# A planner's figures for a transfer through DRAM: later landings and twice the bytes

## The chip, the cores and the metric

The kernel runs on one core of one Trainium2 chip. The metric is the device time of one execution in microseconds (us), lower being better.

## The reference

Gated linear attention feeds a two-layer feed-forward network (FFN). With batch 4, 8 heads, 768 steps and head size 48:

```
for t in range(S):
    state = alpha[:, :, t, :, None] * state + k[:, :, t] (outer) v[:, :, t]
    y[:, :, t] = q[:, :, t] . state
x = y as 3072 tokens x 384
h = x @ w_in                      # 384 x 2048
out = gelu(h) @ w_out             # 2048 x 384
```

## The kernel before

**The attention** is cut into 24 units, numbered n = 2g + u: twelve groups g of 256 steps of one batch, and in each two halves u of four heads. For a unit VectorE (DVE) runs scans over alpha (`pp`, `rp`, lines L315 and L328), multiplies queries and keys by them (`qd` L321, `kd` L334), and TensorE (PE) then makes scores (L355), the part inside a chunk (L445), the new states from keys and values (L464) and the part that comes from older states (L514). ScalarE (ACT) copies the finished `y` out of PSUM (`yc`, L594), so that the bank can be written again.

**The keys have to be turned** for L464. In units 0 to 5 TensorE does it. In units 6 to 23 (`n >= FLIPPED`) DVE transposes 32x32 blocks into `fl` (`flipped`, L371), one DMA writes `fl` to DRAM (`fd`, `flip_out`, L378), four DMAs of 64 KB read it back in another order (`kx`, `flip_back`, L384), and ACT copies `kx` into the tile `kn` that TensorE reads (`flip_over`, L392). `fl` and `kx` have one buffer, `kn` two, `fd` two.

**The FFN** works in float32 with split operands: each weight and each activation is a high and a low part, and three products are summed. Groups 0 to 3 are narrow blocks (256 tokens, first product L622, second L714), the others four wide blocks of 512 tokens (L639, L657). Between the two products ACT does the GELU twice (`ghi` L691, and in place, L695), and DVE takes the difference (`glo` L704).

**The order is made by a planner** that runs when the kernel is built. Every step is an `Op` with an engine, a cost, a list of steps that it depends on and a rank. The planner goes through a time of its own: on each engine it places the step of lowest rank whose inputs are ready; when TensorE has no attention step that is ready, it takes an FFN step. The steps are then issued in the planned order on PE, DVE, ACT and the queue of SyncE (SP). On the chip each engine keeps that order and waits for its semaphores, so the planner's figures set the order and nothing else. For a step that issues transfers, the planner takes one shared bus and a landing time:

```
bus[0] = max(bus[0], o.start) + o.kb / RATE
o.end = (max(o.end, bus[0]) if o.kb else o.end) + o.lands
```

`RATE` is 360 (KB per us of its own count), `WAIT` is 0.2 us between engines, and `o.end` in the second line begins as start plus cost (0.35 for `move`, 1.4 for `moves`). A load of a unit counts 786 KB, or 1179 with the values.

For n from 7 to 12 TensorE's order is the trio outer of n - 2 (L514), inside of n - 1 (L445 and L464), scores of n (L355), issued together; its first step is held back until `kn` of n - 1 is planned as ready, and until keys and queries of n are. Later units keep that hold, with the scores second.

Of the kernel before, what the change touches and what calls it, by code (L numbers as in the profile page):

```python
# [47 lines left out]
def gla_then_gelu_ffn(ctx: ExitStack, tc: tile.TileContext, q, k, v, alpha, qg, kg, ag, vg, w_in, w_out, out):  # L48
# [119 lines left out]
    for half in range(2):  # L168
        r = slice(half * CS, (half + 1) * CS)
# [171 lines left out]
    def scores(g, u):  # L341
        d = cur[g, u]
        n = NU * g + u
        d["s"] = s_of(n)
        if n >= SPLIT:
            d["s"] = [
                ps_h().tile([P, BANK], F32, tag="hp", name=f"sh_{n}"),
                ps_w().tile([P, BANK], F32, tag="sw", name=f"sw_{n}"),
            ]
        for j in range(NCH):  # L350
            for i in range(2):
                t, o = slice(j * CS, (j + 1) * CS), slice(i * CS, (i + 1) * CS)
                for h in range(2):
                    r = slice(h * DP, h * DP + D)
                    nc.tensor.matmul(  # L355
                        d["s"][h][o, t], lhsT=d["kt"][r, (2 * j + i) * CS : (2 * j + i + 1) * CS], rhs=d["qt"][r, i, t], start=True, stop=True
                    )

    def turned(g, u):
        d = cur[g, u]  # L360
        for j in range(NCH):
            e = (2 + j % 2) * C
            nc.tensor.transpose(
                out=d["s"][j // 2][:, e : e + C], in_=d["kt"][:, 2 * j * CS : 2 * (j + 1) * CS], identity=ident
            )

    def flipped(g, u):

        d = cur[g, u]
        d["fl"] = work.tile([P, 4, NCH, QUAD], F32, tag="fl", bufs=1, name=f"fl_{g}_{u}")  # L370
        nc.vector.transpose(  # L371
            out=d["fl"], in_=d["kt"].rearrange("p (j i a t) -> p (i a) j t", j=NCH, i=2, a=2)
        )

    def flip_out(g, u):
        d = cur[g, u]
        d["fd"] = bounce.tile([P, 4, NCH * QUAD], F32, tag="fd", name=f"fd_{g}_{u}")
        nc.sync.dma_start(d["fd"], d["fl"].rearrange("p q j d -> p q (j d)"))  # L378

    def flip_back(g, u):  # L380
        d = cur[g, u]
        d["kx"] = work.tile([P, 4, NCH * QUAD], F32, tag="kx", bufs=1, name=f"kx_{g}_{u}")
        for dst in range(4):
            nc.sync.dma_start(  # L384
                d["kx"][dst * QUAD : (dst + 1) * QUAD],
                d["fd"].rearrange("(s t) q e -> q t s e", t=QUAD)[dst],
            )

    def flip_over(g, u):
        d = cur[g, u]  # L390
        d["kn"] = work.tile([P, 2, NCH, 2, QUAD], F32, tag="kn", bufs=2, name=f"kn_{g}_{u}")
        nc.scalar.copy(  # L392
            d["kn"].rearrange("p h j b d -> p h b j d"),
            d["kx"].rearrange("p (h b) (j d) -> p h b j d", h=2, d=QUAD),
        )
# [476 lines left out]
    def op(*args, **kw):  # L872
        ops.append(Op(*args, **kw))
        return ops[-1]
# [4 lines left out]
    def plan_unit(n):  # L879
        g, u = divmod(n, NU)  # L880
        d = unit[n] = {}
        p, pp_ = unit.get(n - 1, {}), unit.get(n - 2, {})
        r = unit_rank[n]
# [24 lines left out]
        of_y = [yp.get("out", yp.get(x)) for x in ("xh", "xl")]  # L908
        if n >= FLIPPED:
            flip = op("DVE", "flip", lambda: flipped(g, u), [d["keys"], p.get("away")], rank=r)  # L910
            d["away"] = op("SP", "move", lambda: flip_out(g, u), [flip], rank=r - 50, lands=2.2, kb=262)
            back = op("SP", "moves", lambda: flip_back(g, u), [d["away"], p["kn"]], rank=r - 50, lands=2.2, kb=262)
            d["kn"] = op("ACT", "over", lambda: flip_over(g, u), [back, pp_["inside"]], rank=-0.5)
            d["scores"] = op("PE", "scores1", lambda: scores(g, u), [d["keys"], d["q"], sp.get("mask"), sp.get("kn") if n < FLIPPED + NU else None, *shared], rank=r)
        else:
            d["scores"] = op("PE", "scores", lambda: (scores(g, u), turned(g, u)), [d["keys"], d["q"], sp.get("mask"), sp.get("kn"), *shared], rank=r)
# [110 lines left out]
    for n in range(n_units):  # L1027
        plan_unit(n)
# [350 lines left out]
```

## Time and profile before

| | us |
|---|---|
| median of 3 runs | 499.61 (498.85 to 500.62) |
| the profiled execution, its own time | 501.89 |
| its span, first to last instruction | 500.3 |

The profiled execution is one of its own: its time lies 1.59 us above its span, and 2.28 us above the median of the three. Its mean granted TensorE clock is 0.994 of full speed. PE was busy for 483.0 us of the span. The page's busy time of PE is modelled from pipelined matmuls, so idle stretches of PE are read as lost time and busy stretches not as peak.

### The profile page before, as it was taken

Reading aid. Unit: us, or ns where it says so; the run is one execution under the profiler, and the core shown is the slowest. Engines: PE = TensorE matmul, PEld = TensorE weight load, DVE = VectorE, ACT = ScalarE, POOL = GpSimd, SP = SyncE. Lnnn points to the kernel's source line nnn. Section 1 sums busy time; section 2 is a strip of 40 time slices with the busy share of each in tenths; the row PEclk is TensorE's granted clock in tenths of the full one; section 3 lists DMA queues with packets and bytes.
Section 4 is the critical chain, followed back from the end, with each engine's and each line's share of the span. In section 5 each row is a group of like instructions: output and inputs, shape, how many; then the busy total and the mean of one; then the engine's idle time right before and its main releaser. Section 6 shows DMA issues by size and latency. Waiting matters only on the chain.

```text
span 500.3 us, 12076 instructions
## 1 busy us (share of the span) xinstructions
PE 483.0 (97%) x5144; PEld 411.6 (82%) x5144; DVE 261.1 (52%) x503; ACT 201.4 (40%) x399; POOL 7.4 (1%) x21
## 2 busy tenths in 40 slices
PE   7899999998988999999999999999999999999994
PEld 5788998998988998988888777888777888888883
DVE  7998999897877897311111988211532121221212
ACT  5788676434354445231313444222432232332321
POOL 2000000000000000000000000000000000000000
PEclk9999999998999999999999999999999999999998
DMA  8996653755655466100000545000210000100001
GB/s 304 393 346 206 234 190 118 222 180 150 181 171 187 132 195 188 58 33 0 1 0 1 184 157 168 17 0 2 90 41 9 0 1 0 64 1 0 1 0 70
DMA packets 33806, 53.76 MB, mean 107 GB/s; under 512 B 4272, under 2 KB 15344, under 8 KB 33744
## 3 DMA queue, kind: packets, MB, share of 16 engines
q1 hardware_dynamic: 32096, 47.86, 29.3%
q0 software_dynamic: 880, 3.93, 2.0%
q10 hardware_dynamic: 768, 1.11, 0.7%
q8 instruction: 42, 0.69, 0.6%
q14 instruction: 20, 0.16, 0.1%
HBM read 41.29 MB, written 9.44 MB: 101 GB/s over the span
## 4 chain that ended last, share of the span: by engine, by line
PE 72%; DMA 11%; DVE 6%; ACT 5%; SPq 2%; issue 2%; ACTq 0%; DVEq 0%
PE hw L639 27%; PE accw L657 27%; PE acc L714 6%; PE hp L622 5%; DMA st<-in_moe_w_out_dram 2%; DMA kd<-in_kg_dram 2%; DMA x<-z 2%; DMA kx<-fd 2%; PE sbank L514 1%; PE sbank L445 1%; DMA vn<-in_vg_dram 1%; DVE rp L328 1%; SPq L209 1%; ACT ghi L691 1%; PE differ L295 1%
## 5 line engine op out<-in xcount | busy, mean ns | idle before, releaser
L704 DVE TENSOR_TENSOR glo<-hw,ghi 128x512 fp32r<-128x512 f32 x64 | 44.1, 690 | 185.9 <-ACT hw L695 185.9
L639 PE MATMUL hw<-x,wih 128*128 128x512 f32 x384 | 120.9, 395 | 0.0
L691 ACT ACTIVATE ghi<-hw 128x512 fp32r<-128x512 f32 x64 | 38.3, 598 | 171.9 <-PE hw L639 171.9
L639 PEld LDWEIGHTS hw<-x,wih 128*128 128x128 f32 x384 | 71.8, 188 | 17.0
L657 PE MATMUL accw<-ghi,woh 128*128 128x512 f32 x192 | 76.2, 397 | 0.0
L639 PE MATMUL hw<-x,wil 128*128 128x512 f32 x192 | 75.8, 395 | 0.0
L657 PE MATMUL accw<-ghi,wol 128*128 128x512 f32 x192 | 75.2, 392 | 0.0
L622 PE MATMUL hp<-x,wih 128*128 128x256 f32 x384 | 69.7, 282 | 0.0
L622 PEld LDWEIGHTS hp<-x,wih 128*128 128x128 f32 x384 | 59.9, 188 | 0.5 <-issue 0.2
L657 PE MATMUL accw<-glo,woh 128*128 128x512 f32 x192 | 56.2, 394 | 0.0
L622 PE MATMUL hp<-x,wil 128*128 128x256 f32 x192 | 53.6, 280 | 0.0
L714 PE MATMUL acc<-woh,ghi 128*128 128x384 f32 x128 | 45.2, 353 | 0.8 <-ACT ghi L691 0.8
L714 PE MATMUL acc<-wol,ghi 128*128 128x384 f32 x128 | 43.6, 341 | 0.0
L639 PEld LDWEIGHTS hw<-x,wil 128*128 128x128 f32 x192 | 36.0, 187 | 8.9
L657 PEld LDWEIGHTS accw<-ghi,woh 128*128 128x128 f32 x192 | 36.0, 188 | 8.5
L657 PEld LDWEIGHTS accw<-ghi,wol 128*128 128x128 f32 x192 | 36.1, 188 | 7.8
L657 PEld LDWEIGHTS accw<-glo,woh 128*128 128x128 f32 x192 | 35.7, 188 | 7.8
L695 ACT ACTIVATE hw<-hw 128x512 f32<-128x512 f32 x64 | 37.9, 593 | 0.0
L622 PEld LDWEIGHTS hp<-x,wil 128*128 128x128 f32 x192 | 36.2, 188 | 0.0
L328 DVE TENSOR_TENSOR_SCAN rp<-ad,rp,bottom 128x255 f32<-128x255 f32 x48 | 33.9, 738 | 0.8
L315 DVE TENSOR_TENSOR_SCAN pp<-ad,bottom 128x256 f32<-128x256 f32 x48 | 30.8, 667 | 3.8 <-DMA ad<-in_ag_dram 3.8
L704 DVE TENSOR_TENSOR glo<-hp,ghi 128x512 fp32r<-128x512 f32 x30 | 20.6, 687 | 20.8 <-ACT hp L695 20.5
(137 smaller groups left out, 575.3 us busy)
## 6 DMA issues: line engine op xcount, KB each, us to landing
st<-in_moe_w_in_dram SPq DMA_DIRECT2D x8, 768.0 KB, 6.1
st<-in_moe_w_out_dram SPq DMA_DIRECT2D x8, 768.0 KB, 7.7
qd<-in_qg_dram SPq DMA_DIRECT2D x23, 256.0 KB, 4.1
ad<-in_ag_dram SPq DMA_DIRECT2D x23, 256.0 KB, 3.8
kd<-in_kg_dram SPq DMA_DIRECT2D x23, 256.0 KB, 4.8
vn<-in_vg_dram SPq DMA_DIRECT2D x12, 416.0 KB, 6.5
fd<-fl SPq DMA_DIRECT2D x18, 256.0 KB, 2.7
kx<-fd SPq DMA_DIRECT2D x72, 64.0 KB, 3.9
```

Of the source, the lines that this page charges most:

```text
L209: eng.dma_start(data[g % NB][name][:, p].rearrange("p a t -> p (a t)"), src[n])
L295: nc.tensor.matmul(d["to"][i], lhsT=ident, rhs=w[:, i], start=True, stop=False)
L315: nc.vector.tensor_tensor_scan(pp[:, i], at[:, i], bottom, MID, ALU.mult, ALU.max)
L328: nc.vector.tensor_tensor_scan(rp[:, i, G - 2 :: -1], at[:, i, G - 1 : 0 : -1], bottom[:, 1:], rp[:, i, G - 1 :], ALU.mult, ALU.max)
L445: nc.tensor.matmul(ybank[o, i, j * CS : (j + 1) * CS], lhsT=vn[r, j, e : e + rows], rhs=d["ss"][r, h, j, :], start=(j == 0 and i not in sp ...
L622: nc.tensor.matmul(hp[:, j, :], lhsT=a[:, j, i * P : (i + 1) * P], rhs=x[:, i, :], start=(start and m == 0), stop=(stop and (j, i, n) in t ...
L639: nc.tensor.matmul(h, lhsT=a[:, j, i * P : (i + 1) * P], rhs=x[:, i, part], start=(i == 0 and n == 0), stop=(i == NK - 1 and n == 2),)
L657: nc.tensor.matmul(acc[i], lhsT=w[:, j, e], rhs=a, start=(f == 0 and k == 0 and w is wo_hi[f2]), stop=(f == NF - 1 and k == 1),)
L691: nc.scalar.activation(ghi, hp, AF.Gelu)
L695: nc.scalar.activation(hp, hp, AF.Gelu)
L704: nc.vector.tensor_tensor(out=glo, in0=hp, in1=ghi.bitcast(F32), op=ALU.subtract)
L714: nc.tensor.matmul(acc[t], lhsT=a[:, j, t * C : (t + 1) * C], rhs=w[:, j, :], start=(first and j == 0 and k == 0 and w is wo_hi[f]), stop= ...
```

## The change

It changes three numbers that the planner is told. No instruction is added, removed or resized. The write to DRAM (`move`) is told to land 2.6 instead of 2.2 after its end on the bus, the four reads (`moves`) 4.5 instead of 2.2, and the reads count 524 instead of 262 KB on the bus.

```
         if n >= FLIPPED:
             flip = op("DVE", "flip", lambda: flipped(g, u), [d["keys"], p.get("away")], rank=r)
-            d["away"] = op("SP", "move", lambda: flip_out(g, u), [flip], rank=r - 50, lands=2.2, kb=262)
-            back = op("SP", "moves", lambda: flip_back(g, u), [d["away"], p["kn"]], rank=r - 50, lands=2.2, kb=262)
+            d["away"] = op("SP", "move", lambda: flip_out(g, u), [flip], rank=r - 50, lands=2.6, kb=262)
+            back = op("SP", "moves", lambda: flip_back(g, u), [d["away"], p["kn"]], rank=r - 50, lands=4.5, kb=524)
             d["kn"] = op("ACT", "over", lambda: flip_over(g, u), [back, pp_["inside"]], rank=-0.5)
             d["scores"] = op("PE", "scores1", lambda: scores(g, u), [d["keys"], d["q"], sp.get("mask"), sp.get("kn") if n < FLIPPED + NU else None, *shared], rank=r)
```

## Rows read from the trace of the kernel before

**Rows 1.** Page, busy time of an engine, its share of the span, instructions.
```profile
PE 483.0 (97%) x5144; PEld 411.6 (82%) x5144; DVE 261.1 (52%) x503; ACT 201.4 (40%) x399; POOL 7.4 (1%) x21
```

**Rows 2.** Busy time by stretch: start:end, length, engines, PE clock, DMA share, GB/s.
```profile
78.00:211.50 133.50, 128.39 (x2189) 122.37 (x2190) 105.98 (x223) 57.66 (x129) 2.33 (x3) 0.99 0.53 163
211.50:493.50 282.00, 281.96 (x1891) 226.46 (x1889) 85.92 (x162) 85.59 (x165) 2.38 (x4) 1.00 0.11 34
```

**Rows 3.** Page, the chain that ended last, share of the span by engine.
```profile
PE 72%; DMA 11%; DVE 6%; ACT 5%; SPq 2%; issue 2%; ACTq 0%; DVEq 0%
```

**Rows 4.** Waits, 78 to 211 us: waiter and releaser, total us, times, longest.
```profile
ACT kn L392 <- DMA kx<-fd: 30.1, 11, 4.0
...
PE ybank L355 <- ACT yc L594: 1.8, 2, 1.0
...
PE sbank L445 <- ACT yc L594: 1.6, 2, 1.4
...
PE sbank L464 <- ACT kn L392: 1.0, 2, 0.5
...
PE sw L355 <- ACT yc L594: 0.8, 1, 0.8
```

**Rows 5.** The same waits, 211.5 to 493.5 us: ACT's copies of turned keys.
```profile
ACT kn L392 <- DMA kx<-fd: 14.4, 4, 5.2
```

**Rows 6.** Instructions of PE in order of time around unit 9's `kn`.
```profile
115.67 0.65 PE L445 MATMUL sbank<-ss,vn 64*64 64x64 f32 x32
116.84 0.68 PE L464 MATMUL sbank<-vn,kn 64*64 64x48 f32 x32 [0.52 <-ACT kn L392]
118.51 1.13 PE L355 MATMUL ybank<-qd,kd 48*64 48x64 f32 x32 [0.99 <-ACT yc L594]
```

**Rows 7.** Instructions of ACT in the same stretch.
```profile
112.97 0.59 ACT L695 ACTIVATE hp<-hp 128x512 f32<-128x512 f32 x1
116.17 0.62 ACT L392 COPY kn<-kx 128x512 f32<-128x512 f32 x1 [2.61 <-DMA kx<-fd]
116.69 0.72 ACT L217 ACTIVATE junk<-ad,hi_b 128x512 uint8<-128x512 f32 x1
117.32 0.19 ACT L217 ACTIVATION_READ_ACCUMULATOR junk<-ad,hi_b 128x1 f32 x1
117.41 0.57 ACT L691 ACTIVATE ghi<-hp 128x512 fp32r<-128x512 f32 x1
117.89 0.57 ACT L594 COPY yc<-ybank 128x512 f32<-128x512 f32 x1
```

**Rows 8.** Busy time by stretch after these two stalls (columns as in group 2).
```profile
117.00:119.00 2.00, 1.01 (x51) 0.88 (x50) 1.15 (x6) 2.00 (x7) 0.00 (x0) 0.89 0.64 215
119.00:121.00 2.00, 2.00 (x28) 1.88 (x23) 1.98 (x4) 1.07 (x4) 0.00 (x0) 0.50 0.74 237
121.00:123.00 2.00, 2.00 (x11) 2.00 (x11) 0.33 (x2) 0.41 (x2) 0.00 (x0) 0.75 0.58 170
```

**Rows 9.** Issues of SP's queue in order of time, unit 9.
```profile
106.77 0.34 SPq L378 DMA_DIRECT2D fd<-fl  x1
107.15 0.43 SPq L209 DMA_DIRECT2D ad<-in_ag_dram  x1
...
108.61 0.43 SPq L211 DMA_DIRECT2D vn<-in_vg_dram  x1
109.14 2.43 SPq L384 DMA_DIRECT2D kx<-fd  x4
```

**Rows 10.** DMA issues: tiles, queue, count, KB each, median us to landing.
```profile
fd<-fl SPq DMA_DIRECT2D x18, 256.0 KB, 2.7
kx<-fd SPq DMA_DIRECT2D x72, 64.0 KB, 3.9
```

**Rows 11.** The same for the tile `kx` alone, its extremes.
```profile
DMA to landing us min/median/max: 1.8/3.9/7.3
```

**Rows 12.** Instructions of ACT around unit 13's `kn`.
```profile
156.74 0.62 ACT L392 COPY kn<-kx 128x512 f32<-128x512 f32 x1 [2.75 <-DMA kx<-fd]
157.26 0.72 ACT L217 ACTIVATE junk<-ad,hi_b 128x512 uint8<-128x512 f32 x1
...
158.98 0.58 ACT L594 COPY yc<-sbank 128x512 f32<-128x512 f32 x1
```

**Rows 13.** Chain that ended last, one FFN step: start, length, what.
```profile
123.03 2.12 PE hp L622 x18
```

## The prediction

> **What bounds the kernel now.** I read the page's busy times first: PE is busy 97% of the span [rows 1], and the chain that ended last is PE for 72% [rows 3]. A change that adds no PE work can then only move what PE stands idle, so the next view is the table by stretch. From 211.5 to 493.5 us PE is busy 281.96 of 282.00 us: nothing is to be won there. From 78 to 211.5 us it is busy 128.39 of 133.50 [rows 2], which leaves 5.1 us of idle time. Most of the turned units are made here, eleven of the fifteen waits of ACT for them among them [rows 4, 5]. The waits of this stretch name the owners of that idle time: 1.0 us in two waits of PE for ACT's `kn` copies, and 1.8, 1.6 and 0.8 us for ACT's `yc` copies [rows 4]. They sum to 5.2, which is all of it. ACT in turn stood 30.1 us waiting for the `kx` transfers, in eleven waits [rows 4], and 14.4 us more in the later stretch [rows 5], where PE lost nothing. So the wait on ACT has no price of its own. It costs only where something that PE needs soon is queued behind it.
>
> Unit 9 shows both ways of paying. PE had issued the first half of inside (L445) and then stood 0.52 us for `kn`, and after that 0.99 us for `yc` before the scores [rows 6]. On ACT the copy of `kn` began at 116.17 after 2.61 us of idling for `kx`; a range check, a GELU and only then `yc` followed, at 117.89 [rows 7]. Had `kx` come 2.6 us earlier, or had the planner put check and GELU in front of `kn`, `yc` would have been done when PE asked. After the two stalls the granted clock fell to 0.89, 0.50 and 0.75 in three stretches of 2 us [rows 8], that is, to its lower level, 1.2 of 2.4 GHz, for part of them. The loss is (0.11 + 0.50 + 0.25) x 2 = 1.7 us. Unit 13 shows the second way alone: `kn` at 156.74 after 2.75 us of idling, a check, and `yc` at 158.98 [rows 12]; this is the longest wait of L445, 1.4 us [rows 4].
>
> **The change part by part.** No instruction is added or removed, so all of it is order. By the two lines that the planner uses, a write issued at 0 landed at 262/360 + 2.2 = 2.93 before, the reads ended max(1.4, 0.73) + 2.2 = 3.6 later, and with the 0.2 between engines the copy `kn` could be placed 6.73 us after the write's issue. Now it is 0.73 + 2.6 = 3.33, then 1.46 + 4.5 = 5.96, so 9.49: the copy moves back by 2.76 us of the planner's time. Where a load with values (1179 KB, 3.28 us of bus) is issued between write and reads, as in unit 9 [rows 9], the bus term decides in place of the 1.4: before 0.73 + 3.28 + 0.73 + 2.2 = 6.94, now 0.73 + 3.28 + 1.46 + 4.5 = 9.97, a shift of 3.03. On the chip unit 9 took 116.17 - 106.77 = 9.40 us from the issue of the write to the copy [rows 7, 9]. The new figure fits this unit to within 0.6, the old one was 2.5 short, and that is about the 2.61 us that ACT idled [rows 7].
>
> What moves with it. (a) On ACT the copy stands later, so GELUs, checks and `yc` copies that are now queued behind it go in front. (b) On PE the trio is held back until `kn` is planned as ready, and PE takes FFN steps meanwhile. One narrow first product is 2.12 us [rows 13], so a hold of 2.8 is one or two such steps. This is work that PE has to do anyway. If no FFN step were left, the hold would cost its full 2.8 us per unit. Against that speaks that PE goes on with narrow blocks (L622) all through this stretch and then with wide ones for 282 us without a gap [rows 2]; there is stock. (c) The planned landing also delays the loads of a later unit, since they wait for the trio that reads their buffers; they are issued one or two FFN steps later. These loads are outside PE's 5.1 us now, and DVE, which needs them, is busy 105.98 of 133.50 us [rows 2], so it has some 27 us to give. If that slack is used up, PE waits for keys instead; that is the rival on the other side below. (d) The extra 262 KB are 0.73 us of planned bus for the transfers that come after; this only repeats (c) in small.
>
> The sum, for the stretch from 78 to 211.5 us:
> - The two waits for `kn`, 1.0 us [rows 4]: they go, because the copy is planned where it really lands. -1.0.
> - The waits for `yc` behind such copies: 0.99 [rows 6], 0.8 (the only wait of `sw`), and the two of L445, 1.6 [rows 4], together 3.4. The second wait of `ybank` L355, 1.8 - 0.99 = 0.8, stands at the start of the stretch ahead of the first `kn`, so the change does not touch it; it also shows that `yc` can be late without `kx`. Bounds: all 3.4 go, or none. I take two thirds, because unit 9's and unit 13's `yc` have check and GELU behind `kn` that can go ahead [rows 7, 12]. -2.3.
> - The clock: 1.7 us [rows 8] if the pair of stalls of unit 9 goes. The profiled execution is 2.28 us above the median of the runs, so the median may hold this only in part. I take half, with bounds 0 and 1.7. -0.9.
> - New stalls. No row shows them. The lower bound is nothing, as in the long later stretch [rows 2], and the upper is the cost of one such pair with its clock, 0.52 + 0.99 + 1.7 = 3.2 [rows 6, 8]. A new order of some hundred steps does not come out without any; I take two of the size of unit 9's first, +1.0.
>
> That makes -3.2 us: 499.61 - 3.2 = 496.4 for the median. Against the profiled execution's own time the clock counts in full, 501.89 - 4.0 = 497.9, with a span near 496.3.
>
> The Trainium skill, "DMA: Bandwidth & Descriptors", section "Anatomy of one DMA", would speak against the change: it gives a transfer a fixed 2.0 us plus its bytes at 436 GB/s (its fit is for another issuing path). By that an estimate for a read of 64 KB is 2.15 us and for the write of 256 KB 2.6 us, so 2.2 would have been right for the reads and 4.5 a needless hold, and the sum would be 0. Here the write's median of 2.7 agrees [rows 10]; the reads' median of 3.9 does not, and only their minimum of 1.8 comes near it, with 7.3 at the other end [rows 11].
>
> **The rivals.**
> - *Paid back, or too late for nothing (no change).* The wait on ACT falls, but PE's idle time only changes its place, as in the later stretch, where 14.4 us on ACT cost PE nothing [rows 5]. For it: only 5.2 of 30.1 us on ACT reach PE [rows 4], and reads that land in 1.8 us [rows 11] make a hold planned for 4.5 empty. Against: the two waits for `kn` are direct. In this case the copy still runs before PE asks, a few stalls of 0.5 to 1 us replace others, and the time is 499.6 give or take 1.2.
> - *The held trio makes keys late (slower).* A trio held back by 2.8 us frees its buffers as much later, the next unit's load goes out as much later, and the scans of DVE start late; then PE stands at the scores (L355) for `kd`. Its price is that of unit 9, stall and clock, 3.2 us each time [rows 6, 8]. If the old stalls go as well (-4.4 and up to -1.7), it takes two such places to come out even and three for +3.5; if the old `yc` stalls stay, one or two are enough, for 501.5 to 503. Against it: DVE's 27 us of slack [rows 2].
> - *Everything goes (much faster).* All of 1.0 + 3.4 + 1.7 = 6.1 us, with no new stall: 493.5.
>
> **How the numbers follow.** Less than 0.3%, 1.5 us, can't be told from no change here: faster is below 498.1 and slower above 501.1. The forecast, 494.5 to 498.1, gets 0.45; everything gone, 0.13; no change, 0.25; keys late, 0.17. So faster is 0.58, same 0.25, slower 0.17. The likeliest time is 496.4. The range begins with the case in which everything goes, 493.5, and ends inside the slower case, at 501.6; some 0.08 is left out below and 0.11 above.
>
> **What would show it.** Right: ACT's idle time for `kx` from 78 to 211 falls from 30.1 to less than 15 us; PE's waits for `kn` are gone and those for `yc` are below 2 us; PE's idle time in the stretch is 2 to 3 us, and the clock is 1.00 from 115 to 125. More FFN steps stand between two trios in units 8 to 12. Wrong: PE waits at L355 for `kd`, or the clock falls in another place (keys late); the idle total stays near 5 us under other names (paid back); or PE shows idle time before an FFN step, which would mean that the stock ran out.

## The result, and the profile after

| | before | after |
|---|---|---|
| median, us | 499.23 (497.68 to 500.62, 4 runs) | 493.60 (493.41 to 493.84, 4 runs) |
| ratio of the times | | 0.9888, 95% interval 0.9858 to 0.9919 |
| span of the profiled execution | 500.3 | 492.1 |

The change made the kernel 1.1% faster, 5.6 us between the medians. The runs of the changed kernel lie within 0.4 us, those of before over 2.9 us.

The page of the changed kernel, busy time by engine:

```profile
PE 480.8 (98%) x5144; PEld 410.2 (83%) x5144; DVE 262.5 (53%) x503; ACT 202.1 (41%) x399; POOL 7.4 (2%) x21
```

Its busy time by stretch (columns as in group 2 of the rows above):

```profile
0.00:78.00 78.00, 73.59 (x1099) 63.84 (x1099) 69.41 (x122) 59.44 (x109) 2.68 (x14) 1.00 0.77 276
78.00:211.50 133.50, 133.50 (x2194) 126.82 (x2195) 108.11 (x224) 58.91 (x131) 3.06 (x4) 1.00 0.53 166
211.50:485.30 273.80, 273.72 (x1854) 219.57 (x1852) 84.31 (x158) 83.79 (x161) 1.66 (x3) 1.00 0.11 34
```

and, as it was not shown above, the first stretch of the kernel before:

```profile
0.00:78.00 78.00, 72.67 (x1066) 62.82 (x1066) 68.51 (x120) 58.13 (x106) 2.67 (x14) 1.00 0.77 276
```

In the stretch from 78 to 211.5 us PE no longer stands idle at all: 133.50 of 133.50, where it was 128.39 [rows 2]. Of the 8.2 us between the two spans, 5.1 are this: 4.4 in waits behind copies of `kn` [rows 4], 0.4 in the wait at the head of the stretch and 0.3 in a wait of an FFN step for `glo`. The clock's 1.7 us [rows 8] are gone as well, and 5.33 - 4.41 = 0.9 us of idle time fell away before 78 us. That makes 7.7. PE's busy time fell by 483.0 - 480.8 = 2.2 us, 0.5 more than the clock's part; no view shows why. The 0.9 us before 78 are no gain of the change: nearly all of that stretch lies ahead of the first turned unit, and in the experiments below the same idle time is anything from 4.0 to 6.0 us.

The waits of the changed kernel, 78 to 211.5 us, hold one row of those of [rows 4]:

```profile
ACT kn L392 <- DMA kx<-fd: 8.2, 4, 3.0
```

ACT idles 8.2 us for the reads instead of 30.1, in four waits instead of eleven, and the four kinds of PE's waits for `kn` and `yc` are gone. Unit 9 again, PE and then ACT in order of time:

```profile
119.29 0.34 PE L714 MATMUL acc<-woh,ghi 128*128 128x384 f32 x1
119.47 0.34 PE L714 MATMUL acc<-wol,ghi 128*128 128x384 f32 x1
119.74 0.67 PE L514 MATMUL ybank<-qd,state 48*48 48x64 f32 x32
120.22 0.65 PE L445 MATMUL sbank<-ss,vn 64*64 64x64 f32 x32
120.69 0.63 PE L464 MATMUL sbank<-vn,kn 64*64 64x48 f32 x32
121.16 0.69 PE L355 MATMUL ybank<-qd,kd 48*64 48x64 f32 x32
```

```profile
116.31 0.60 ACT L691 ACTIVATE ghi<-hp 128x512 fp32r<-128x512 f32 x1 [5.54 <-PE hp L622]
116.80 0.59 ACT L695 ACTIVATE hp<-hp 128x512 f32<-128x512 f32 x1
117.32 0.60 ACT L392 COPY kn<-kx 128x512 f32<-128x512 f32 x1
...
120.53 0.59 ACT L594 COPY yc<-ybank 128x512 f32<-128x512 f32 x1 [0.91 <-PE ybank L514]
```

The trio now stands behind more FFN work (between it and the trio before it 36 products of L622 and 32 of L714, where it was 36 and 12) and runs without a gap. The copy of `kn` begins 3.4 us before PE asks for it (117.32 to 120.69) and is done in 0.6; before, PE stood waiting for it [rows 6]. On ACT a pair of GELUs went ahead of the copy, and `yc` waits for PE's outer step instead of PE waiting for `yc`. The clock through this place is whole, where it was 0.89, 0.50 and 0.75 [rows 8]:

```profile
117.00:119.00 2.00, 2.00 (x17) 2.00 (x17) 1.65 (x3) 1.50 (x4) 0.00 (x0) 1.00 0.65 252
119.00:121.00 2.00, 2.00 (x93) 1.75 (x94) 0.86 (x2) 1.09 (x4) 0.00 (x0) 1.00 0.27 76
121.00:123.00 2.00, 2.00 (x63) 1.93 (x56) 1.50 (x5) 0.83 (x3) 0.00 (x0) 1.00 0.24 64
```

### The profile page after: what moved, and what is told of

The parts are those of the page before. It is cut to its first block, busy times and chain, and to the rows that moved or that the text cites. A ratio compares the mean times of both kernels' runs of the same rounds, so it can differ in the third digit from the quotient of the medians.

```text
span 492.1 us, 12092 instructions
## 1 busy us (share of the span) xinstructions
PE 480.8 (98%) x5144; PEld 410.2 (83%) x5144; DVE 262.5 (53%) x503; ACT 202.1 (41%) x399; POOL 7.4 (2%) x21
## 4 chain that ended last, share of the span: by engine, by line
PE 88%; DVE 5%; DMA 3%; ACT 2%; issue 1%; POOL 1%; ACTq 0%; SPq 0%; POOLq 0%
PE hw L639 27%; PE accw L657 27%; PE acc L714 11%; PE hp L622 10%; DMA st<-in_moe_w_out_dram 2%; PE sbank L445 2%; PE sbank L514 2%; PE sbank L464 1%; PE differ L295 1%; PE sh L355 1%; DVE rp L328 1%; PE ybank L514 1%; DVE st L273 1%; DVE pp L315 1%; PE ybank L355 0%
## 5 line engine op out<-in xcount | busy, mean ns | idle before, releaser
L622 PE MATMUL hp<-x,wih 128*128 128x256 f32 x384 | 69.5, 281 | 0.0
L622 PEld LDWEIGHTS hp<-x,wih 128*128 128x128 f32 x384 | 59.8, 188 | 0.4 <-issue 0.2
L622 PE MATMUL hp<-x,wil 128*128 128x256 f32 x192 | 53.6, 280 | 0.0
L714 PE MATMUL acc<-woh,ghi 128*128 128x384 f32 x128 | 44.1, 345 | 0.8 <-ACT ghi L691 0.8
L714 PE MATMUL acc<-wol,ghi 128*128 128x384 f32 x128 | 43.1, 336 | 0.0
L622 PEld LDWEIGHTS hp<-x,wil 128*128 128x128 f32 x192 | 36.2, 188 | 0.0
L691 ACT ACTIVATE ghi<-hp 128x512 fp32r<-128x512 f32 x32 | 19.1, 596 | 41.4 <-PE hp L622 41.4
```

What stands on the lines that cost most here:

```text
L622: nc.tensor.matmul(hp[:, j, :], lhsT=a[:, j, i * P : (i + 1) * P], rhs=x[:, i, :], start=(start and m == 0), stop=(stop and (j, i, n) in t ...
L691: nc.scalar.activation(ghi, hp, AF.Gelu)
L714: nc.tensor.matmul(acc[t], lhsT=a[:, j, t * C : (t + 1) * C], rhs=w[:, j, :], start=(first and j == 0 and k == 0 and w is wo_hi[f]), stop= ...
```

## The experiments

Two questions were open. Is the late copy of `kn` really what PE paid for, and which half of the new order pays, ACT's or PE's? And is it the size of the shift that counts, or would any new order have gained? "PE idle" below is the length of the stretch from 78 to 211.5 us less PE's busy time in it, "ACT for kx" the wait of ACT's copy in the same stretch, both from one profiled execution; the median and its ratio to the kernel before come from several runs. Where the profiled execution is far from the median (the table at the end has both), its idle time is not that of the median.

**The wait taken away, all orders kept.** The copy of `kn` reads `fl`, a tile that is already in SBUF. The waits of this and the following kernels are shown for the stretch from 78 to 211.5 us, as waiter and releaser, total us, times, longest.

```
-            d["kx"].rearrange("p (h b) (j d) -> p h b j d", h=2, d=QUAD),
+            d["fl"].rearrange("p (h b) j d -> p h b j d", h=2),
```

> The kernel before, in which ACT's copy into kn reads fl instead of kx (the turned keys are then in the wrong places; all transfers still run). The order on PE, DVE and SP is that of the kernel before, so only ACT's wait for the reads is taken away. Theory (the copy waits for transfers that land later than planned, and PE pays for what stands behind it): PE's idle time from 78 to 211 us falls from 5.2 to under 1.5 us, the clock stays at 1.00, and the time is 493.5 to 496. Rival (the gain is luck of a new order, the waits for kx are harmless): PE's waits for yc stay, 498.5 to 500.

Measured: 495.15 us, ratio 0.9903 (0.9870 to 0.9935). PE idle 133.50 - 132.88 = 0.6 us. PE's waits in the stretch:

```profile
PE ybank L355 <- ACT yc L594: 0.3, 1, 0.3
...
PE acc L714 <- DVE glo L704: 0.3, 1, 0.3
```

The order on PE and DVE is that of the kernel before, to the instruction, and nearly the whole gain is there. So its stalls came from the copy's wait for the reads, also those that the trace puts down to `yc`, which does not read `kx`.

**The two halves of the new order, each alone.** Each of the two kernels moves the copies in its plan after it is made, and the order on PE, DVE and SP stays. The fence shows the lines of both kernels together (the comments are not in them): the first kernel, on the plan of before, has the third line and not the fourth; the second, on the plan of the change, has the fourth and not the third. The first never puts a copy behind the step that reads it, so it moves the copies of units 9 and 11 by 2.0 us only.

```
+    for n in range(FLIPPED, n_units):
+        o, first = unit[n]["kn"], unit[n]["inside"]
+        o.start = min(o.start + 2.8, first.start - 0.01)      # plan of before
+        o.start = max(o.start - 2.8, first.start - 1000)      # plan of the change
     plan.sort(key=lambda o: (o.start, o.n))
```

> The plan of the kernel before, with ACT's copies into kn put 2.8 us later in ACT's order alone (never behind inside); PE, DVE and SP keep the order of the kernel before. Theory: PE's two waits for kn stay or grow (1.0 to 2 us), those for yc fall from 3.4 to about 1.5 us, as GELU and check are now ahead of the copy; 496.5 to 498.5. Rival (PE's held trio does all of it): nothing gained, 499 to 501, with PE waiting longer for kn.

Measured: 497.00 us, ratio 0.9934 (0.9910 to 0.9959). PE idle 2.0 us. ACT for kx, and what is left of PE's waits for it:

```profile
ACT kn L392 <- DMA kx<-fd: 2.0, 1, 2.0
...
PE sbank L464 <- ACT kn L392: 1.3, 1, 1.3
...
PE ybank L464 <- ACT kn L392: 0.2, 1, 0.2
```

> The plan of the changed kernel, with ACT's copies into kn put 2.8 us earlier in ACT's order alone; PE, DVE and SP keep the order of the changed kernel. Theory: ACT idles for kx more than 20 us again between 78 and 211 us, PE has no wait for kn, since its trio is held back, and waits for yc of 0.5 to 1.5 us in sum; 494 to 496. Rival (ACT's order does all of it): PE's waits for yc are back at 3 us, 496.5 to 498.5.

Measured: 494.31 us, ratio 0.9898 (0.9845 to 0.9950). PE idle 0.2 us, and

```profile
ACT kn L392 <- DMA kx<-fd: 18.1, 8, 5.4
...
PE acc L714 <- DVE glo L704: 0.2, 1, 0.2
```

ACT's order alone takes away all waits for `yc`, as (a) said, and more of them than expected; but with PE's order of before the copy is now late for PE, with one wait of 1.3 us. PE's held trio alone (with the new order on DVE and SP) takes away both kinds, though ACT idles 18.1 us for `kx`. The two halves don't add up (0.66% and 1.02%, together 1.1%): either takes away most of the stalls, and the held trio leaves less, 0.2 us of idle time against 2.0.

**The three numbers one by one.** In `move` and `moves`: reads 4.5 alone; bytes 524 alone; write 2.6 alone.

> Only the 4.5 for the reads; the write lands at 2.2 and the reads count 262 KB, as before. By the planner's lines the copy moves back 2.3 us of the 2.76. Theory: nearly all of the gain, 493.5 to 495.5. Rival (a chance order): anywhere between 494 and 501, with PE's idle time at other places.

Measured: 495.36 us, ratio 0.9911 (0.9883 to 0.9939); PE idle 0.3, ACT for kx 10.5. As the theory said. (PE idle here is a wait of an FFN step for `glo`.)

> Only the 524 KB for the reads; both landings stay at 2.2. By the planner's lines the copy moves back 0.06 us where no load stands between write and reads (the bus takes 1.46 and the issues 1.4) and 0.73 where one does. Theory: the copies stay far ahead of the transfers, ACT still idles over 20 us for kx between 78 and 211 us, and PE keeps stalls behind them: 497 to 500. Rival (any new order gains, the order of before is an unlucky one): 494 to 496 with ACT's waits unchanged.

Measured: 494.82 us, ratio 0.9895 (0.9860 to 0.9929); PE idle 0.35 us, and

```profile
ACT kn L392 <- DMA kx<-fd: 12.7, 9, 2.8
...
PE ybank L355 <- ACT yc L594: 0.5, 2, 0.3
```

A miss: the bytes alone bring all that can be told from the change itself. Either any new order would do, or a shift of less than 1 us is already enough.

> Only the 2.6 for the write. The copy moves back 0.4 us. Theory: as for the bytes alone, 497.5 to 500, with ACT's waits for kx over 20 us and stalls of PE of 3 us or more between 78 and 211 us. Rival (unlucky order of before): 494 to 496.

Measured: 498.62 us, ratio 0.9982 (0.9954 to 1.0010), no difference that these runs can tell. PE idle 2.0 us, nearly all of it in waits for `yc` (one of 1.0 in unit 9's trio and one of 0.8 in unit 11's), and ACT for kx 27.1. This is hardly a new order, though: the plan puts the copies of units 6 to 11 where they were, because in those units other steps and transfers decide and not the write's landing, and the trace has the order of before on PE, ACT and DVE up to 143 us. Its two waits are there in the kernel before too, of the same length; the two waits for `kn` in front of them (0.5 us each before) are missing in this execution. So the run does not decide between any new order and a short shift.

**The size of the shift, smaller and in the other direction, and a control.** The reads' landing alone at 1.5, 2.6 and 3.0 instead of 2.2; then, with the figures for the keys as before, `lo=1.0` instead of `lo=0.89` in the table of costs.

> Only the reads' landing, at 1.5 instead of 2.2: the copies move 0.7 us the other way. Theory (the margin between copy and trio sets the stalls): PE stalls for kn and yc grow over the 5.2 us of the kernel before, ACT idles over 30 us for kx between 78 and 211 us, 499.5 to 502.5. Rival (any new order gains): 494 to 497.

Measured: 502.53 us (498.66 to 503.98), ratio 1.0046 (1.0011 to 1.0080): half a per cent slower. The profiled execution took 500.30, 2.2 below the median, with PE idle 3.5 us in the stretch and 1.4 us behind it (a wait of a wide block's second product for a GELU, at 290 us), so the stalls of 5.2 or more were not seen. What the other executions lost shows in part in the granted clock: its mean over the span is 0.994 or less in five of the seven, and 0.988 or 0.989 in three, where the profiled one has 0.998. ACT for kx rose as expected:

```profile
ACT kn L392 <- DMA kx<-fd: 37.4, 13, 6.7
...
PE ybank L355 <- ACT yc L594: 1.7, 3, 1.0
...
PE sw L355 <- ACT yc L594: 1.5, 1, 1.5
...
PE sbank L464 <- ACT kn L392: 0.6, 2, 0.3
```

> Only the reads' landing, at 2.6 instead of 2.2, a shift of the copies of 0.4 us. Theory: part of the gain, PE's stalls between 78 and 211 us 1 to 3 us, 495.5 to 498.5. Rival (any new order gains): 494 to 495.5.

Measured: 496.24 us, ratio 0.9917 (0.9883 to 0.9950); PE idle 2.6, ACT for kx 19.4. The profiled execution took 499.85, 3.6 above the median, so most executions lose less than this one. One trio (unit 11's `kn`, then `yc`) makes 2.1 us of the idle time, and the clock fell behind it, just as in the kernel before:

```profile
137.00:139.00 2.00, 0.86 (x38) 0.73 (x41) 0.67 (x3) 2.00 (x6) 0.00 (x0) 1.00 0.68 176
139.00:141.00 2.00, 2.00 (x36) 1.93 (x32) 1.52 (x6) 1.29 (x4) 0.00 (x0) 0.71 0.99 351
141.00:143.00 2.00, 2.00 (x8) 2.00 (x7) 1.93 (x4) 0.03 (x1) 0.00 (x0) 0.50 0.58 158
143.00:145.00 2.00, 2.00 (x17) 2.00 (x17) 1.03 (x2) 0.00 (x0) 0.00 (x0) 0.94 0.13 39
```

> Only the reads' landing, at 3.0 instead of 2.2, a shift of the copies of 0.8 us, about what the doubled bytes alone gave. Theory: the gain of the bytes alone, 494 to 495.5, PE's stalls under 1 us. Rival (the gain of the bytes came from the other transfers' bus): PE's stalls of 2 us or more, 496 to 499.

Measured: 495.45 us, ratio 0.9902 (0.9870 to 0.9934). PE idle 1.2, of which 0.9 is one wait for a GELU and 0.3 for `yc`; ACT for kx 17.4. SP's order is that of the bytes alone, and PE's, ACT's and DVE's differ from it in a few places. So the doubled bytes act as a shift of some 0.8 us. The two plans agree: in units 6 to 13 both put the copies 0.7 to 2.3 us later after their write than before, within 0.1 us of each other. The arithmetic for the bytes, 0.06 to 0.73, leaves out what the order that follows from them moves.

> A control: the figures for the turned keys as before, and another cost of the planner changed (the low part of a weight on DVE 1.0 instead of 0.89), so that the order of all later steps is new. Theory: the copies are planned as early after the write as before, ACT idles over 20 us for kx between 78 and 211 us, and PE keeps stalls for kn and yc of 2 us or more: 497 to 501. Rival (the order of before was an unlucky one and any new one gains): 494 to 496.

Measured: 498.20 us, ratio 0.9965 (0.9940 to 0.9990). ACT for kx stays at 26.5. Of PE's stalls one of 1.0 us is left, fewer than expected: part of what the kernel before paid was the luck of its order, but this control gains a third of a per cent against 1.1. The control does not price that luck cleanly: its PE idle time, 1.2 us, is that of the kernel with reads at 3.0, and its median is 2.75 us longer all the same. PE is busy 482.6 us in it and 480.8 in the other:

```profile
PE 482.6 (97%) x5146; PEld 411.4 (83%) x5146; DVE 262.1 (53%) x503; ACT 202.8 (41%) x399; POOL 7.4 (1%) x21
PE 480.8 (97%) x5144; PEld 410.0 (83%) x5144; DVE 262.3 (53%) x503; ACT 202.7 (41%) x399; POOL 7.4 (1%) x21
```

Why is not shown. So how much another order would gain with the copies planned as early as before stays open.

**Too much of it.** The reads told to land at 6.8, and at 12.0, with the other two numbers as in the change.

> The changed kernel with the reads told to land at 6.8 instead of 4.5, another 2.3 us. Theory (the hold is filled with FFN steps, and the stock does not run out): ACT's waits for kx go to nearly nothing, PE's idle time from 78 to 211 us stays under 1 us; 493 to 494.5, as the changed kernel. Rival (a hold longer than the landing makes keys late): PE waits for kd or other steps of DVE, 495 to 498.

Measured: 495.16 us, ratio 0.9904 (0.9876 to 0.9932). PE idle 0.4, no wait of ACT for `kx`. The median is 0.7 above what was expected; its interval overlaps that of the change, and PE shows no wait for keys.

> The changed kernel with the reads told to land at 12.0 instead of 4.5, another 7.5 us. Theory: by now the loop trio, load, scans, keys, flip, write, reads, copy, trio is the longest, so units come at longer intervals; but PE fills them with FFN steps of the narrow and the first wide block, and the tail has slack, so 493 to 495.5. Rival (keys late, or the x of a later block late): PE idles before FFN steps or at L355, 496 to 505.

Measured: 494.57 us, ratio 0.9897 (0.9854 to 0.9940). The stretch of this kernel:

```profile
78.00:211.50 133.50, 133.24 (x1830) 126.93 (x1827) 87.60 (x176) 52.50 (x114) 3.05 (x4) 1.00 0.40 123
```

DVE did 87.6 us of work in it instead of 108.1: a good part of the attention has moved behind 211.5 us. PE idles 0.3 us all the same.

All in the order of the shift. It is taken from the plan that each kernel makes: the time from the write's issue to the copy, as the mean of units 6 to 18 (those of the stretch), is 7.33 us in the kernel before, and the second column is how much later than that the copies stand. "Idle later" is PE's idle time from 211.5 to 485.3 us, "profiled" the time of the profiled execution, to which both idle times and ACT's wait belong. Each ratio is to runs of the kernel before on the same chip, whose medians were 499.98 to 500.34 us in the three sets of experiments:

| told | copies later by, us | ACT for kx | PE idle | idle later | profiled | median | ratio |
|---|---|---|---|---|---|---|---|
| reads 1.5 | -0.9 | 37.4 | 3.5 | 1.4 | 500.30 | 502.53 | 1.0046 |
| before | 0 | 30.1 | 5.1 | 0.0 | 501.89 | 499.23 | 1 |
| write 2.6 | 0.0 | 27.1 | 2.0 | 0.7 | 498.39 | 498.62 | 0.9982 |
| control | +0.1 | 26.5 | 1.2 | 0.0 | 498.33 | 498.20 | 0.9965 |
| reads 2.6 | +0.4 | 19.4 | 2.6 | 0.2 | 499.85 | 496.24 | 0.9917 |
| bytes alone | +0.7 | 12.7 | 0.35 | 0.3 | 495.12 | 494.82 | 0.9895 |
| reads 3.0 | +0.9 | 17.4 | 1.2 | 0.8 | 496.55 | 495.45 | 0.9902 |
| reads 4.5 | +2.2 | 10.5 | 0.3 | 0.0 | 495.23 | 495.36 | 0.9911 |
| the change | +3.0 | 8.2 | 0.0 | 0.1 | 493.65 | 493.60 | 0.9888 |
| reads 6.8 | +6.0 | none | 0.4 | 0.0 | 495.35 | 495.16 | 0.9904 |
| reads 12.0 | +11.0 | none | 0.3 | 0.0 | 494.62 | 494.57 | 0.9897 |

Copies planned earlier cost; 0.4 us later they bring most of the gain; from 0.7 us on all ratios lie between 0.989 and 0.991, and their intervals overlap. The order of before without the wait for `kx` has 0.9903: that, and not the control, shows that the waits for the reads are what PE paid for.

## Why the prediction was right, and where its sizes were off

The direction and the mechanism were right, and 493.6 lies inside the range, but hardly: it is the time of the case "everything goes" (493.5), which had 0.13, and lies outside the forecast of 494.5 to 498.1, which had 0.45. The forecast of -3.2 us was short by 2.4, and PE's idle time, forecast at 2 to 3 us, is 0.

- *Copies planned later* (the two lines of the planner, 2.76 us): right in kind. ACT's wait fell below the 15 us that were named. The mean shift of the plans is 3.0. But so much was not needed; some 0.8 does the same. The sum for a unit with a load in between leaves out the 0.2 us between engines that the other sum has: with it the new figure is 10.17, 0.8 above the 9.40 measured in unit 9, and the old one 7.14, 2.3 short. The planner itself has 12.14 and 7.77 for this unit, because the load starts 2.7 and 1.4 us behind the write's issue and not at once. For the bytes the working had 0.73 us and called it small; that misled.
- *The two waits for `kn`, -1.0*: right, both gone.
- *The waits for `yc`, -2.3 of 3.4*: mis-sized, all 3.4 are gone. The reason given for two thirds, GELU and check going ahead on ACT, holds (ACT's order alone removed them), but the sum overlooked that step (b) removes them too: with the trio held back, the same late ACT has caught up by the time PE asks. With two covers, each enough for these waits by itself, the full amount was the likelier one.
- *The 0.8 us at the head of the stretch, left standing*: the same wait stands ahead of the stretch in the changed kernel, 0.2 us long, and is 0.3 in the kernel without the wait for `kx`, whose PE order is that of before. So its size differs between executions, and that is no gain of the change. It also means that the waits named in the prediction, 5.2, are not quite the 5.1 of the stretch: 0.5 of this wait lies before 78 us, and 0.3 is a wait for `glo` that was not named.

```profile
78.39 0.69 PE L355 MATMUL ybank<-qd,kd 48*64 48x64 f32 x32 [0.86 <-ACT yc L594]
77.30 0.69 PE L355 MATMUL ybank<-qd,kd 48*64 48x64 f32 x32 [0.22 <-ACT yc L594]
```

- *The clock, -0.9*: gone in the profiled execution, 1.7 us. For the other executions the mean granted clock of each tells more. In 25 of 52 executions of the kernel before, on three chips, it is 0.990 to 0.994; in all 42 of the changed kernel and of the kernels with no wait for `kx`, with the held trio alone or with copies 0.7 us or more later it is 0.995 to 0.999. The loss of full-speed time, (1 - clock) x span, is 2.6 us against 1.6 on the mean; what both have lies at the end (in the changed kernel the clock falls by 488 to 490 us, when PE is done). So the clock gave back 1.0 us on the mean, and the half that was taken fits. How the rest of the 5.6 us divides over the stalls is known for the one profiled execution alone.
- *New stalls, +1.0*: wrong for this order, there are none. Other new orders do come with some: 0.9 us for a GELU with reads at 3.0, and in six of the kernels 0.2 to 1.4 us in the wide blocks, at 285 to 290 us, where the kernel before has none.
- *The stock of FFN steps* (b) and *DVE's slack* (c): right, and with more room than was claimed: even copies planned 11 us later leave PE 0.3 us idle. So the rival "keys late" is not only absent here; the runs at +6.0 and +11.0 did not bring it about. Its price was added up wrongly: with the `yc` stalls left, -1.0 + 3.2 makes 501.8 for one place and -1.0 + 6.4 makes 505.0 for two, not 501.5 to 503.
- *Paid back (no change)*: refuted by the kernel without the wait for `kx`, and by the row of shifts from 0.4 us on.
- *The Trainium skill's fixed cost* in "DMA: Bandwidth & Descriptors", section "Anatomy of one DMA", by which 2.2 was right for the reads and 4.5 a needless hold, did not decide. Told 3.0 the kernel was faster than told 2.2 (0.9902), and told 1.5 slower (1.0046). That 4.5 holds longer than needed is so; the hold is free.

## What to carry to other kernels

Where a planner fixes the order of in-order engines, tell it landing times on the late side wherever the engine that bounds the kernel has other work to fill the hold: too early costs a stall of everything behind the waiting instruction, too late cost nothing here that can be told, up to 11 us. Look for the price not at the wait itself (30 us on ACT) but at what the bounding engine next needs from the engine that waits (5 us for `kn` and `yc`). To learn whether a wait matters, feed the waiting instruction from data that is there already and keep all orders.

## What the runs showed of the hardware

The granted clock of TensorE fell to its lower level, 1.2 of 2.4 GHz, after two stalls close to each other: 0.52 and 0.99 us [rows 6, 8], and 1.61 and 0.51 us in the kernel with reads at 2.6, each time with a loss of 1.7 us of full-speed time ((0.29 + 0.50 + 0.06) x 2 in the latter). With reads at 1.5 the pairs of 0.33 and 0.99 us and of 0.28 and 1.50 us left it at 1.00. So a pair of short stalls of PE can cost about twice its length, but need not.

The 72 reads of the changed kernel landed between 1.8 and 9.1 us after their issue, a wider spread than before [rows 11], though only the order of the issues had changed, and neither their number nor their size (one execution of each kernel):

```profile
DMA to landing us min/median/max: 1.8/3.4/9.1
```
